# A fused attention and MLP kernel: casting loads gated on q instead of v, the query indicator on another queue, and small parameter work moved from VectorE to GpSimd

## The chip, the cores and the metric

One core of a Trainium2 chip runs the whole kernel. The metric is the device time of one execution in microseconds (us). The engines are TensorE (PE, with its weight loads shown apart as PEld), VectorE (DVE), ScalarE (ACT), GpSimd (POOL) and SyncE (SP); each works through its own instructions in order and waits for others by semaphores. DMAs are issued from the queues of SP, ACT and GpSimd. Only DMAs issued from GpSimd change a type on the way here ("casting loads", float32 in memory to bfloat16 or float16 on chip); those from SP and ACT copy as is.

## The reference

Attention with a block mask over q, k and v of shape [4, 8, 768, 64], then a residual MLP over the result, seen as x of shape [4, 768, 512]:

```python
scores = scale * np.matmul(q, k.transpose(0, 1, 3, 2))
# mask: neighbouring blocks of 32, first and last block, three sampled blocks per block row
scores = np.where(mask, scores, -1000000000.0)
attn = softmax(scores)
x = heads side by side of np.matmul(attn, v)
a1 = alpha1 * x + beta1
u = x + lam * (w_tok @ a1)          # over the 768 positions
a2 = alpha2 * u + beta2
out = u + lam * (np.maximum(a2 @ w_ch1, 0.0) @ w_ch2)
```

## The kernel before, in words

The work is cut into 16 pairs of heads (4 batches, 4 pairs each). A pair has 9 units; a unit is a set of score matmuls for 128 keys by 512 queries twice (line 576, `emit_qk`), one exponential over 128x1024 on ACT (line 594, `emit_exp`), and the product of the exponentials with v on PE (line 623, `emit_pv`). The score tile `sp` has two buffers, so the scores of unit s wait for the exponential of unit s-2.

For the first 5 pairs the mask is part of the score matmul: below the 64 rows of q stand 24 rows that tell the block of each query (the **query indicator**, `indq_c`, loaded by DMA into `qTs` at lines 350 and 362), and below the 64 rows of k stand 24 rows of a mask term (`kTs`, lines 426 and 432: `emit_mask_part` and the copies `rows1` to `rows3`). No score matmul can run before the indicator has landed in its buffer. Later pairs multiply by `mask01`, which GpSimd builds piece by piece (line 512).

The order is written out. A loop over the first 45 units (line 1012) emits, for each step s, the scores, the exponential, at some steps the loads of a later pair, then the small jobs whose date in the table `PLAN` has the whole part s and a fraction below 0.5, then the product with v of unit s-2, then the jobs with a fraction of 0.5 or more. The table `ENG` says on which engine a small copy runs (0 VectorE, 1 ScalarE, 2 GpSimd). After step 45 the strings `WEAVE` give the order. As every engine runs in the emitted order, a date decides what an instruction stands behind.

The start, which the change touches:

- Lines 345 to 364 issue the first DMAs: q, k and v of the first pair, head by head (`load_first`, line 341, 192 KB each), the sampled blocks, the constants (identity and static mask, 80 KB), the query indicator (72 KB, once for each of two buffers) and the rows of lam, alpha1 and beta1 (`vrows`).
- On GpSimd, lines 373 to 380 make `pick` from the identity (it waits for the constants), and line 382 copies one column of the first v into `gate`. This copy does nothing but wait: the casting loads that follow it on GpSimd's queue (`emit_load`, line 304) don't start before that v has landed.
- `emit_parts` (lines 679 to 683) splits the 12 rows of `vrows` into three bfloat16 parts with five small instructions, on VectorE. `emit_bcast` (line 688) multiplies `pick` with the parts on PE, which spreads lam, alpha1 or beta1 over 128 partitions, and VectorE evicts it (lines 697 and 699). These feed `a1pp` (lines 655 and 656) on GpSimd.
- `emit_tps0` transposes q and k of the first pair on PE (line 474), `emit_tps` those of pairs 1 to 4 (line 486); VectorE evicts them (lines 464 and 492). `emit_wtk_load` (line 738) loads the token weights, which PE transposes (line 744) from step 11 on.
- `emit_warm` (line 456) issues PE matmuls on zeros at the start, in the gaps.

Of the kernel before, what the change touches and what calls it, by code (L numbers as in the profile page):

```python
# [16 lines left out]
ALU = mybir.AluOpType  # L17
# [54 lines left out]
]  # L72
WEAVE = W1 + W2 * (B - 2) + W3
ENG = {
    "layv00": 0,
    "layv01": 0,
    "layk01": 0,
    "layq01": 0,
    "kT0": 0,
    "qT0": 0,  # L80
    "kT1": 0,
    "qT1": 0,
    "mp0": 1,
    "mp1": 1,
    "mp2": 0,
    "rows1": 0,
    "rows2": 0,
    "rows3": 0,
    "parts": 0,
    "tk1": 0,  # L90
    "tq1": 0,
}
# [2 lines left out]
    "wtkl": 0.42,  # L95
    "warm1": 0.49,
    "loadv2": 0.58,
    "mask_cols": 1.6,
    "layk01": 1.22,
    "layq01": 1.25,  # L100
    "rows2": 4.5,
    "rows1": 2.08,
    "parts": 2.83,
    "tps0": 2.82,
    "mask1": 2.94,
    "w1_0": 2.96,
    "warm2": 3.04,
    "layv01": 4.3,
    "warm0": 3.31,
    "bcast0": 4.1,  # L110
    "tq1": 3.8,
    "tk1": 4.82,
    "bcast2": 5.12,
    "rows3": 5.84,
    "lv1": 6.01,
    "loadk3": 6.08,
    "loadv3": 6.92,
    "mask3": 7.41,
    "bcast1": 7.8,
    "loadk2": 8.21,  # L120
    "loadq3": 8.23,
    "loadq2": 8.52,
    "a1pp0": 9.37,
    "w1_2": 9.64,
    "w1_1": 10.3,
# [11 lines left out]
    "wt3": 15.31,  # L137
    "columns_use": 16.32,
    "tk2": 16.6,
    "tok0_0": 16.75,  # L140
    "tok0_1": 17.4,
    "tk3": 18.13,
    "loadk4": 18.23,
# [16 lines left out]
    "lv4": 25.4,  # L160
    "tok1_1": 25.6,
    "tok1_2": 27.2,
    "loadv5": 27.51,
    "tok1_3": 27.74,
    "tok1_4": 28.91,
    "tok1_5": 29.7,
# [1 line left out]
    "mask5": 30.09,  # L168
    "tq4": 30.41,
    "mask15": 30.72,  # L170
    "tk4": 30.72,
    "udma0": 31.32,
    "udma1": 31.9,
    "w2_1": 32.0,
    "tq5": 32.01,
    "mask9": 32.65,
    "tok2_0": 33.91,
    "tk5": 34.64,
# [5 lines left out]
    "mask11": 35.79,  # L184
    "tok2_3": 36.37,
    "lam16": 37.24,
    "mask16": 37.75,
    "tok2_4": 37.77,
    "mask10": 37.9,
    "tok2_5": 38.61,  # L190
    "w2_3": 38.7,
    "tok3a_0": 38.84,
    "tok3a_1": 38.93,
    "tok3a_2": 39.02,
    "tok3a_3": 39.35,
    "tok3b_0": 39.51,
    "tok3b_1": 39.52,
    "tok3b_2": 39.53,
    "tok3b_3": 39.54,
    "mask17": 39.68,  # L200
    "ut2": 39.85,
    "tok3a_4": 39.98,
    "mask12": 40.23,
    "tok3b_4": 40.23,
    "usc1": 40.28,
    "lv5": 40.42,
    "tok3a_5": 40.52,
    "ut3_0": 40.8,
    "tok3b_5": 41.21,
    "cast3": 42.22,  # L210
    "lam3": 43.09,
    "ut3_1": 43.63,
    "lam1": 44.85,
    "lam10": 44.92,
    "lam7": 45.27,
    "lam0": 45.32,
    "lam11": 45.58,
    "lam6": 45.9,
    "lam13": 46.09,
    "lam2": 46.25,  # L220
    "lam5": 47.61,
    "lam14": 47.82,
    "lam4": 47.9,
    "lam9": 48.25,
    "lam12": 49.8,
    "lam8": 50.02,
    "lam15": 50.13,
}

# [2 lines left out]
def kernel(  # L232
# [16 lines left out]
    nc = tc.nc  # L249
# [30 lines left out]
    def ptile(shape, dt, name):  # L280
        return pp.tile(shape, dt, name=name, tag=name)
# [4 lines left out]
    def copy_of(name):  # L286
        return (nc.vector.tensor_copy, nc.scalar.copy, nc.gpsimd.tensor_copy)[ENG[name]]

    NVB = 3
    vexts = [ptile([P, 2, NT, D + 1], F16, f"vext{i}") for i in range(NVB)]  # L290
    raws = {}

    def emit_load(i, which="qkv"):
        b, hp = i // NP, i % NP
        for nm, src, dt in (("q", q, BF), ("k", k, BF), ("v", v, F16)):
            if nm not in which or (i, nm) in raws:
                continue
            if nm == "q":
                t = qpads[i % 2][:, D : D + 2 * NT * D].rearrange(
                    "p (w x) -> p w x", w=2  # L300
                )
            else:
                t = ap_.tile([P, 2, NT * D], dt, name=nm + "r", tag=nm + "r", bufs=2)[:]
            nc.gpsimd.dma_start(
                t, src[b, 2 * hp : 2 * hp + 2].rearrange("w (p o) d -> p w (o d)", o=NT)
            )
            raws[(i, nm)] = t
# [18 lines left out]
    identb = const[:, 0:P]  # L326
# [13 lines left out]
    def load_first(nm, src, w, eng):  # L340
        eng.dma_start(  # L341
            raws[(0, nm)][:, w, :], src[0, w].rearrange("(p o) d -> p (o d)", o=NT)
        )
# [2 lines left out]
    load_first("k", k, 0, nc.scalar)  # L346
    nc.sync.dma_start(sampi[0:NBLK, :], sampled_blocks.bitcast(I32))
    nc.scalar.dma_start(const[:], const_dr.ap())
    load_first("v", v, 0, nc.sync)
    nc.sync.dma_start(  # L350
        qTs[0][D : D + NBLK], indq_dr.ap().rearrange("r (w s) -> r w s", w=2)
    )
    load_first("k", k, 1, nc.scalar)
    load_first("q", q, 1, nc.sync)
    load_first("v", v, 1, nc.sync)
# [15 lines left out]
        nc.gpsimd.memset(t[:, QS * D :], 0.0)  # L371

    pick = ptile([P, 12], BF, "pick")
    for m in (32, 64):
        nc.gpsimd.tensor_tensor(
            out=pick[0:96],
            in0=identb[0:96, 0:12] if m == 32 else pick[0:96],
            in1=identb[0:96, m : m + 12],
            op=ALU.add,
        )  # L380
    gate = ptile([P, 1], FP, "gate")
    nc.gpsimd.tensor_copy(out=gate[:], in_=raws[(0, "v")][:, 0, 0:1])
    expb = ptile([P, 1], FP, "expb")
    nc.vector.memset(expb[:], EXPB)

# [2 lines left out]
    for o in (slice(0, 4), slice(4, NT)):  # L388
# [6 lines left out]
        out=eqt,  # L395
        in0=rndf[0:NBLK, :].unsqueeze(2).broadcast_to([NBLK, NR, NBLK]),
        in1=eqt,
        op=ALU.is_equal,
# [8 lines left out]
        out=mbs[0:NBLK, :],  # L407
        in0=mbm[0:NBLK, :],
# [8 lines left out]
    def emit_mask_part(jp, copy):  # L417
        sl = kText[0][D : D + NBLK, ts(jp, 2 * P)]
        dst = sl.rearrange("q (o g r) -> q o g r", o=2, r=16)
        src = mbs[0:NBLK, :].rearrange("q (g m) -> q g m", m=3)  # L420
        m_of = (6 * np.arange(16) + 2 * jp) // BLK
        assert (m_of == (6 * np.arange(16) + 2 * jp + 1) // BLK).all()
        for m in range(3):
            lo, hi = np.searchsorted(m_of, [m, m + 1])
            shape = [NBLK, 2, NBLK // 3, int(hi - lo)]
            copy(
                out=dst[:, :, :, int(lo) : int(hi)],
                in_=src[:, :, m].unsqueeze(1).unsqueeze(3).broadcast_to(shape),
            )
# [241 lines left out]
    parts = ptile([P, P], BF, "parts")  # L671
    part = ptile([P, P], BF, "part")
    rest = ptile([P, P], FP, "rest")
    nc.gpsimd.memset(parts[:], 0.0)

    def emit_parts():
        r = slice(0, 12)
        eng = (nc.vector, None, nc.gpsimd)[ENG["parts"]]
        eng.tensor_copy(out=parts[r], in_=vrows[r])
# [237 lines left out]
            start_mlp(i // NP)  # L917

    emit_load(1)
    emit_mask_part(0, copy_of("mp0"))  # L920
    emit_mask_part(1, copy_of("mp1"))
    emit_tps0(0)
# [192 lines left out]
```

## Time and profile before

| | us |
|---|---|
| median of 3 runs | 308.48 (308.0 to 308.75) |
| the profiled execution | 308.91 |
| its span | 306.7 |
| PE busy in the span | 300.1 |
| ACT busy | 213.5 |
| DVE busy | 200.6 |
| GpSimd busy | 105.1 |
| VectorE's five parts instructions, first to last start | 10.98 to 12.76 |
| score matmuls of the first unit start | 6.71 |

The profile takes one execution. Its page gives each engine's busy time, the chain that ended last, and groups of instructions by line. Queries of the trace give the same for stretches of the span, the instructions in order of time, and, for each wait, who ended it: "A <- B: 0.9, 1, 0.9" says that A's engine sat idle 0.9 us in all, once, at most 0.9, until B. In a row of the table of stretches stand the stretch, its length, the busy time of PE, PEld, DVE, ACT and POOL with the number of instructions, the granted TensorE clock (1.00 throughout), the DMA share and what the DMAs moved. In a row in order of time stand the start, the duration, engine, line, operation, and in brackets the idle time before it and what ended that.

### The profile page before, as it was taken

The numbers are of one execution on the slowest core, as the hardware profiler recorded it, in microseconds if no ns is written. First come the engines' busy times: TensorE is split into PE (matmuls) and PEld (weight loads), VectorE is DVE, ScalarE is ACT, GpSimd is POOL, SyncE is SP. The second block draws the span as 40 slices with busy tenths as digits, with TensorE's granted clock in tenths as the row PEclk, the third lists the DMA queues.
The fourth block names the chain that finished last, engine by engine and source line by source line (L and its number), as shares of the span: only waits on it lengthen the run. The fifth ranks groups of instructions, "written<-read, shape, count | busy, mean of one in ns | idle before, by whom it ended". The sixth has DMA issues, their size and how long they took to land.

```text
span 306.7 us, 7685 instructions
## 1 busy us (share of the span) xinstructions
PE 300.1 (98%) x3225; PEld 188.3 (61%) x3225; DVE 200.6 (65%) x373; ACT 213.5 (70%) x314; POOL 105.1 (34%) x141
## 2 busy tenths in 40 slices
PE   7899999999999999999999999999999999999995
PEld 3577888666575756556665655557565765555543
DVE  4887889889776887478686668477786664000111
ACT  4799998999797946869988565869888521454210
POOL 3759598452252161162434600262222200000000
PEclk9999999999999999999999999999999999999999
DMA  5999999962574299353665995344701023000011
GB/s 182 167 197 204 203 161 164 150 108 42 107 113 84 61 126 204 92 82 82 86 116 108 157 116 85 95 73 73 109 36 26 36 60 89 9 34 34 36 68 68
DMA packets 56293, 31.00 MB, mean 101 GB/s; under 512 B 36352, under 2 KB 53140, under 8 KB 56132
## 3 DMA queue, kind: packets, MB, share of 16 engines
q0 software_dynamic: 16608, 14.22, 31.8%
q1 hardware_dynamic: 39220, 15.83, 24.7%
q8 instruction: 25, 0.41, 0.5%
q10 hardware_dynamic: 432, 0.48, 0.5%
q14 instruction: 8, 0.07, 0.1%
HBM read 29.86 MB, written 6.29 MB: 118 GB/s over the span
## 4 chain that ended last, share of the span: by engine, by line
PE 94%; ACT 2%; DMA 1%; DVE 1%; issue 0%; SPq 0%; DVEq 0%
PE mm L829 27%; PE mm L848 26%; PE mm L761 11%; PE sp L576 11%; PE op L623 11%; PE mm L576 4%; ACT eT L594 2%; DMA qTs<-indq_c 1%; PE mm L868 1%; PE mm L623 1%; PE mm L486 1%; PE mm L744 1%; PE mm L791 1%; SPq L341 0%; DVE qTs L464 0%
## 5 line engine op out<-in xcount | busy, mean ns | idle before, releaser
L594 ACT ACTIVATE eT<-sp,expb 128x1024 f16<-128x1024 f32 x111 | 119.1, 1119 | 6.1 <-PE sp L576 5.7
L836 ACT ACTIVATE hts<-mm 128x384 bf16<-128x384 f32 x128 | 60.7, 498 | 51.7 <-PE mm L829 51.7
L829 PE MATMUL mm<-uT,w1b 128*128 128x384 bf16 x512 | 95.3, 326 | 0.0
L848 PE MATMUL mm<-w2b,hts 128*128 128x512 bf16 x368 | 90.6, 379 | 0.0
L611 DVE TENSOR_TENSOR eT<-eT,mask 128x1024 f16<-128x1024 f16 x99 | 75.8, 780 | 20.5 <-ACT eT L594 20.2
L655 POOL TENSOR_TENSOR a1pp<-x_sb,vbc 128x384 bf16<-128x384 f32 x27 | 29.9, 1107 | 124.9 <-DVE x_sb L641 99.3
L829 PEld LDWEIGHTS <-w1b 128*128 128x128 bf16 x512 | 47.3, 98 | 31.6 <-issue 0.9
L623 PEld LDWEIGHTS <-eT 128*128 128x128 f16 x1152 | 47.5, 98 | 18.6 <-issue 5.0
L594 ACT ACTIVATE eT<-mm,expb 128x512 f16<-128x512 f32 x66 | 41.7, 684 | 19.0 <-PE mm L576 18.9
L848 PEld LDWEIGHTS <-hts 128*128 128x128 bf16 x368 | 33.1, 98 | 32.2 <-issue 1.5
L623 PE MATMUL op<-vext,eT 128*128 128x65 f16 x1008 | 47.4, 194 | 0.1
L857 DVE TENSOR_TENSOR ot<-x_sb,mm 128x512 f32<-128x512 f32 x23 | 15.7, 684 | 41.0 <-PE mm L848 41.0
L761 PE MATMUL mm<-a1pp,wtokT 128*128 128x128 bf16 (+1 forms) x612 | 39.7, 216 | 0.0
L761 PEld LDWEIGHTS <-wtokT 128*128 128x128 bf16 x612 | 34.7, 98 | 4.6 <-ACT hts L836 1.0
L576 PE MATMUL sp<-qTs,kTs 88*128 88x512 bf16 (+1 forms) x120 | 26.9, 325 | 1.3 <-ACT eT L594 0.5
L656 POOL TENSOR_TENSOR a1pp<-a1pp,vbc 128x384 bf16<-128x384 bf16 x27 | 27.2, 1008 | 2.1
L776 DVE TENSOR_TENSOR x_sb<-x_sb,mm 128x384 f32<-128x384 f32 x32 | 17.6, 549 | 11.4 <-PE mm L761 10.8
L576 PE MATMUL sp<-qhT,khT 64*128 64x256 bf16 (+1 forms) x198 | 20.4, 305 | 0.0
L576 PEld LDWEIGHTS <-khT 64*128 64x128 bf16 x264 | 11.3, 94 | 14.7 <-issue 9.2
L782 DVE CAST ubf<-x_sb 128x384 bf16<-128x384 f32 x32 | 17.7, 553 | 1.1
L641 DVE TENSOR_TENSOR x_sb<-op,rcp 128x384 f32<-128x384 f32 x28 | 15.6, 557 | 1.0
L640 DVE RECIPROCAL rcp<-op 128x6 f32<-128x6 f32 x28 | 5.4, 191 | 13.0 <-PE op L623 13.0
(86 smaller groups left out, 184.1 us busy)
## 6 DMA issues: line engine op xcount, KB each, us to landing
out_dram<-ot SPq DMA_DIRECT2D x23, 256.0 KB, 3.0
qpad<-in_q_dram POOLq DMA_DIRECT2D x15, 192.0 KB, 3.8
kr<-in_k_dram POOLq DMA_DIRECT2D x15, 192.0 KB, 5.2
vr<-in_v_dram POOLq DMA_DIRECT2D x15, 192.0 KB, 5.7
w1b<-in_moe_w_ch_dram POOLq DMA_DIRECT2D x4, 512.0 KB, 10.6
w2b<-in_moe_w_ch_dram POOLq DMA_DIRECT2D x4, 512.0 KB, 7.8
hts<-in_moe_w_tok_dram POOLq DMA_DIRECT2D x1, 1152.0 KB, 11.5
x_sb<-in_k_dram ACTq DMA_DIRECT2D x2, 192.0 KB, 3.4
```

The costliest lines, as they stand in the source:

```text
L576: nc.tensor.matmul(sp[jj][:, dst], lhsT, rhs, start=True, stop=True, skip_group_check=True,)
L594: nc.scalar.activation(dst, at, AF.Exp, bias=expb[:], scale=SCALE)
L611: nc.vector.tensor_mul(out=e, in0=e, in1=keep)
L623: nc.tensor.matmul(op[0][:, o, :], ets[u][:, jj, h * QB + n * P : h * QB + n * P + P], vexts[i % NVB][:, w, 2 * jp + jj, :], start=op[1] == 0,
L655: eng.tensor_tensor(out=dst, in0=x_sbs[b][:, :, cols], in1=bc[0], op=ALU.mult)
L656: eng.tensor_tensor(out=dst, in0=dst, in1=bc[1], op=ALU.add)
L761: nc.tensor.matmul(ps[:, o % 3, cols], wtokT[:, os_, ts(o, P)], a1pps[i][:, os_, cols], start=(os_ == 0 and o % 3 == 0 and half != 1), sto ...
L776: nc.vector.tensor_tensor(out=x, in0=x, in1=ps[:], op=ALU.add)
L782: nc.vector.tensor_copy(out=ubfs[i][:, sl, :], in_=x_sbs[b][:, sl, ts(hp, P)])
L829: nc.tensor.matmul(ps[:, 0:QC], w1b[:, dk, ts(n, P)], uTs[b][:, dk, ts(c, QC)], start=(dk == 0), stop=(dk == 3),)
L836: nc.scalar.activation(hts[(b, c)][:, n, :], ps[:, 0:QC], AF.Relu)
L848: nc.tensor.matmul(ps[:], ht[:, nk, ts(o % 3, P)], w2b[:, nk, :], start=(nk == 0), stop=(nk == NH - 1),)
```

## The change

Six things are done:

1. The first query indicator is issued from ACT's queue, third there (after the first k and the constants, ahead of the second head's k), instead of fourth on SP's queue.
2. `gate` copies from the first q instead of the first v.
3. `pick` (two instructions) and the memset of `parts` are emitted after the casting loads of pair 1 instead of before them.
4. The five parts instructions and the copy `rows2` run on GpSimd instead of VectorE.
5. The three broadcasts have their dates one step later, the transposes `tps0` of the second head half a step earlier within step 2, and the copy of pair 1's v (`lv1`) one step earlier.
6. Some dates after step 16 move: the first token job behind the step's products, transposes of pairs 4 and 5 by half a step to one step, some jobs of pairs 2 and 3 by half a step, one load of w2 ahead of pair 6's casting loads, some mask and lam jobs.

The core of the diff:

```diff
     "mp2": 0,
+    "parts": 2,
...
-    "rows2": 0,
+    "rows2": 2,
...
-    "parts": 0,
...
-    "tps0": 2.82,
+    "tps0": 2.52,
     "parts": 2.83,
...
-    "bcast0": 4.1,
-    "bcast2": 5.12,
-    "lv1": 6.01,
+    "lv1": 5.01,
+    "bcast0": 5.1,
+    "bcast2": 6.12,
-    "bcast1": 7.8,
-    "loadq3": 8.23,
+    "bcast1": 8.8,
+    "loadq3": 9.23,
...
-    "tok0_0": 16.75,
+    "tok0_0": 17.05,
...
-    "tk4": 30.72,
+    "tk4": 31.72,
-    "tq5": 32.01,
+    "tq5": 32.51,
...
-    "w2_3": 38.7,
+    "w2_3": 37.7,
...
     nc.scalar.dma_start(const[:], const_dr.ap())
-    load_first("v", v, 0, nc.sync)
-    nc.sync.dma_start(
+    nc.scalar.dma_start(
         qTs[0][D : D + NBLK], indq_dr.ap().rearrange("r (w s) -> r w s", w=2)
     )
+    load_first("v", v, 0, nc.sync)
     load_first("k", k, 1, nc.scalar)
...
-    for m in (32, 64):
-        nc.gpsimd.tensor_tensor(
-            out=pick[0:96],
-            in0=identb[0:96, 0:12] if m == 32 else pick[0:96],
-            in1=identb[0:96, m : m + 12],
-            op=ALU.add,
-        )
     gate = ptile([P, 1], FP, "gate")
-    nc.gpsimd.tensor_copy(out=gate[:], in_=raws[(0, "v")][:, 0, 0:1])
+    nc.gpsimd.tensor_copy(out=gate[:], in_=raws[(0, "q")][:, 0, 0:1])
...
-    nc.gpsimd.memset(parts[:], 0.0)
...
     emit_load(1)
+    for m in (32, 64):
+        nc.gpsimd.tensor_tensor(
+            out=pick[0:96],
+            in0=identb[0:96, 0:12] if m == 32 else pick[0:96],
+            in1=identb[0:96, m : m + 12],
+            op=ALU.add,
+        )
+    nc.gpsimd.memset(parts[:], 0.0)
     emit_mask_part(0, copy_of("mp0"))
```

More of the change, by code (lines that the diff above doesn't have):

```diff
@@ L74 @@
 ENG = {
+    "kT0": 0,
+    "kT1": 0,
+    "layk01": 0,
+    "layq01": 0,
     "layv00": 0,
     "layv01": 0,
[L77 to L82, printed above, removed]
     "mp0": 1,
@@ L85 @@
     "mp2": 0,
+    "parts": 2,
+    "qT0": 0,
+    "qT1": 0,
     "rows1": 0,
-    "rows2": 0,
+    "rows2": 2,
     "rows3": 0,
-    "parts": 0,
     "tk1": 0,
@@ L97 @@
     "loadv2": 0.58,
-    "mask_cols": 1.6,
     "layk01": 1.22,
     "layq01": 1.25,
-    "rows2": 4.5,
+    "mask_cols": 1.5,
     "rows1": 2.08,
+    "tps0": 2.52,
     "parts": 2.83,
-    "tps0": 2.82,
     "mask1": 2.94,
@@ L107 @@
     "warm2": 3.04,
+    "warm0": 3.31,
+    "tq1": 3.8,
     "layv01": 4.3,
-    "warm0": 3.31,
-    "bcast0": 4.1,
-    "tq1": 3.8,
+    "rows2": 4.5,
     "tk1": 4.82,
-    "bcast2": 5.12,
+    "lv1": 5.01,
+    "bcast0": 5.1,
     "rows3": 5.84,
-    "lv1": 6.01,
     "loadk3": 6.08,
-    "loadv3": 6.92,
+    "bcast2": 6.12,
+    "loadv3": 7.02,
     "mask3": 7.41,
-    "bcast1": 7.8,
     "loadk2": 8.21,
-    "loadq3": 8.23,
     "loadq2": 8.52,
+    "bcast1": 8.8,
+    "loadq3": 9.23,
     "a1pp0": 9.37,
@@ L162 @@
     "tok1_2": 27.2,
-    "loadv5": 27.51,
+    "loadv5": 27.53,
     "tok1_3": 27.74,
@@ L170 @@
     "mask15": 30.72,
-    "tk4": 30.72,
-    "udma0": 31.32,
+    "udma0": 30.82,
+    "tk4": 31.72,
     "udma1": 31.9,
-    "w2_1": 32.0,
-    "tq5": 32.01,
+    "w2_1": 32.02,
+    "tq5": 32.51,
     "mask9": 32.65,
@@ L186 @@
     "lam16": 37.24,
+    "mask17": 37.68,
+    "w2_3": 37.7,
     "mask16": 37.75,
@@ L189 @@
     "mask10": 37.9,
-    "tok2_5": 38.61,
-    "w2_3": 38.7,
[L192 to L195, printed above, removed]
+    "tok3a_0": 38.34,
+    "tok3a_1": 38.43,
+    "tok2_5": 38.51,
+    "tok3a_2": 38.52,
+    "tok3a_3": 38.85,
+    "tok3a_4": 39.48,
     "tok3b_0": 39.51,
@@ L199 @@
     "tok3b_3": 39.54,
-    "mask17": 39.68,
     "ut2": 39.85,
-    "tok3a_4": 39.98,
+    "tok3a_5": 40.02,
     "mask12": 40.23,
@@ L206 @@
     "lv5": 40.42,
-    "tok3a_5": 40.52,
     "ut3_0": 40.8,
@@ L210 @@
     "cast3": 42.22,
+    "lam2": 42.25,
     "lam3": 43.09,
@@ L214 @@
     "lam10": 44.92,
+    "lam9": 45.25,
     "lam7": 45.27,
@@ L219 @@
     "lam13": 46.09,
-    "lam2": 46.25,
     "lam5": 47.61,
@@ L223 @@
     "lam4": 47.9,
-    "lam9": 48.25,
+    "lam8": 49.72,
     "lam12": 49.8,
-    "lam8": 50.02,
     "lam15": 50.13,
```

## The prediction

> **What bounds the kernel now.** I read the page first. Its line of busy time puts PE at 300.1 of 306.7 us, and the chain that ended last is PE for 94%. So the span is PE's work plus PE's idle time, and an edit can gain only where PE idles. The second view, the table of stretches, says where that is.
>
> ```profile
> PE 300.1 (98%) x3225; PEld 188.3 (61%) x3225; DVE 200.6 (65%) x373; ACT 213.5 (70%) x314; POOL 105.1 (34%) x141
> ```
> ```profile
> core 0: us, PE busy (x) PEld busy (x) DVE busy (x) ACT busy (x) POOL busy (x), PEclk, DMA share, GB/s
> 0.00:4.60 4.60, 3.41 (x8) 1.04 (x8) 0.85 (x5) 1.73 (x3) 0.94 (x12) 1.00 0.53 166
> 4.60:6.71 2.11, 1.69 (x10) 0.88 (x9) 1.95 (x8) 1.24 (x7) 0.71 (x4) 1.00 0.82 267
> ...
> 8.50:10.81 2.31, 2.12 (x14) 1.05 (x14) 1.80 (x6) 2.31 (x3) 2.31 (x5) 1.00 1.10 163
> 10.81:13.19 2.38, 1.44 (x27) 1.17 (x28) 2.19 (x7) 1.55 (x2) 1.87 (x3) 1.00 1.21 168
> 13.19:15.79 2.60, 2.43 (x38) 1.85 (x39) 2.53 (x6) 1.38 (x3) 0.70 (x1) 1.00 0.97 199
> 15.79:20.29 4.50, 4.03 (x54) 2.76 (x54) 4.25 (x10) 4.50 (x5) 1.67 (x3) 1.00 1.11 199
> 20.29:30.00 9.71, 9.71 (x161) 8.03 (x160) 7.19 (x17) 8.90 (x9) 9.44 (x12) 1.00 1.27 204
> ```
>
> Length less PE busy is PE's idle time. From 20.29 on it is nothing until the last 6.7 us. Between 4.60 and 20.29 it is 0.42, 0.09 (the row left out), 0.19, 0.94, 0.17 and 0.47, together 2.28 us: the most that this change can win, since the end of the kernel is not touched. The third view, the waits of the first 30 us, names two of these by cause, and ACT's loss beside them.
>
> ```profile
> ACT eT L594 <- PE sp L576: 3.7, 6, 1.2
> ...
> PE mm L688 <- DVE parts L683: 0.9, 1, 0.9
> ...
> PE sp L576 <- DMA qTs<-indq_c: 0.4, 1, 0.4
> ```
>
> The fourth view, the instructions in order of time, shows the two places: the first score matmuls at 6.71 come 0.42 us late for the query indicator; the broadcast at 13.19 waits for five small DVE instructions that begin at 10.98, and the next scores (13.99) stand behind it, so that ACT, idle from 13.40, begins its sixth exponential only at 14.63.
>
> ```profile
> 6.71 0.59 PE L576 MATMUL sp<-qTs,kTs 88*128 88x512 bf16 x2 [0.42 <-DMA qTs<-indq_c]
> ...
> 10.98 0.21 DVE L679 CAST parts<-vrows 12x128 bf16<-12x128 f32 x1
> ...
> 12.29 1.11 ACT L594 ACTIVATE eT<-sp,expb 128x1024 f16<-128x1024 f32 x1 [0.82 <-PE sp L576]
> ...
> 13.19 0.38 PE L688 MATMUL mm<-parts,pick 96*128 96x128 bf16 x4 [0.94 <-DVE parts L683]
> ...
> 14.63 8.18 ACT L594 ACTIVATE eT<-sp,expb 128x1024 f16<-128x1024 f32 x8 [1.23 <-PE sp L576]
> ```
>
> Eight exponentials then run end to end to 22.81: there ACT paces PE, and afterwards PE is full.
>
> **The change, part by part.**
>
> *Query indicator on ScalarE's queue.* SP issued it fourth at 2.08; ACT issues it third, in the slot that began at 1.67. The last landing moves from 6.67 to at most 6.26 by the issue alone, and earlier if it no longer stands behind the first v (192 KB). PE's two warm-up matmuls end at 6.29 and the weight load had begun at 6.10, so PE starts there: gain 0.42. ACT's queue pays one more issue of 0.40 to 0.48, which puts its table load at 2.65 to 3.93; the cast behind it waited for k until 4.16, so 0.23 of cover is left. The second head's k is issued 0.48 later; its cast is not before 7.44, and the first k took 3.4 us from issue to landing, so it is there near 5.6 plus the 72 KB now ahead of it. SP's later DMAs each move up by about 0.4.
>
> *Parts to GpSimd, broadcast 0 behind the sixth scores.* DVE loses 0.21+0.28+0.59+0.56+0.28 = 1.92 us, plus one rows copy of 0.35. On PE the order becomes scores 4, values, k transposes, scores 5, broadcast 0. Before, from 11.65: scores 4, stall, broadcast, values (8 matmuls), transposes, scores 5 ending at 14.59. Now, everything 0.43 earlier: scores 4 at 11.22, done 11.82; the pieces take 0.43, 0.25 and 0.34 on PE by the chain, so scores 5 begin near 12.24 and are done at 12.84. Exponential 4 starts at 11.86 and lasts 1.11 to 12.97; exponential 5 follows at once. It was at 14.63: **1.66 us earlier**, of which 0.42 is the indicator, 0.94 the stall, and about 0.30 the broadcast's own PE time, now under ACT-paced scores. The broadcast's work of 0.24 to 0.38 moves into 12.7 to 21, where PE had 0.64 of idle time for it.
>
> *Do the parts come in time?* GpSimd before: gate at 6.21, then three casting loads 0.89, 0.71, 0.71 apart, the token weights 0.55, three loads at 0.70 each, the mask copy at 11.45. Now the gate waits for q, which DVE's first cast got at 3.99. The loads go out from about 4.15; picks (0.29 each), memset, weights and three loads follow, and the parts start at 9.8. No row has these five on GpSimd. Low bound: 0.20 each as the 96x12 add, 1.0 in all. High: 1.1 each as the 128x384 multiply, 5.5. Nearest rows are the mask copy (240 elements, 0.60) and that multiply scaled to 128 columns: 0.38 for the three copies and 0.55 for the two subtractions, 2.25 in all, done at 12.1. PE wants them at 12.7. A later finish costs nothing until 12.9 (broadcast 0.24, values 0.25, scores 0.6, against exponential 6 at 14.0); from there it costs one for one. The end runs from 10.8 to 15.3, so the cost from 0 to 2.4.
>
> [...]
>
> *Gate on q.* The three loads go out 2.3 us earlier; they landed no sooner than 3.8, 4.1 and 5.6 us after issue, so pair 1 is in by about 8.0, 9.2 and 11.4, against PE's wants at 10.9 (q) and 11.9 (k) and DVE's near 14 (v). The token weights took 11.5 us and PE waited 0.16 for them at 20.29. They are issued at 7.15 instead of 8.78 and stand behind data that is 2.2 earlier: landing 18.1 to 18.7, and PE's want moves to 18.5. So this part gains nothing by itself; it keeps the weights from taking back the 1.66. Their possible cost is 0 to 0.2.
>
> *Rows 2 on GpSimd.* 768 columns, 0.8 to 2.0 us by the same rows, after the first w1 issue: done by 16 at the latest, wanted by the tenth scores near 17. GpSimd had waited 1.78 and 3.46 us at 12.7 to 18.6, which hides this and the parts. *Values 1 a step earlier, and dates after step 16* (token jobs, transposes of pairs 4 and 5 by half a step to a step, one w2 load ahead of pair 6's loads): PE is full there and no work is added; cost nothing, with the cover that the buffers are written steps ahead; if it fails, a rival below.
>
> **Sum.** 0.42 + 0.94 + 0.30 = 1.66 us. The profiled execution took 308.91 (span 306.7 and 2.2 around it) and would take 307.25. The median of the runs is 308.48, 0.43 below that execution; so the median after is 306.8, rounded to **306.9** for the weights' 0 to 0.2.
>
> **Rivals.** What a measurement of this kernel can tell is about 0.3%, 0.93 us: faster means under 307.55.
>
> 1. *Parts late on GpSimd* (that engine becomes the bound). With the two rows unscaled (three copies at 0.60, two subtractions at 1.1) they take 4.0, end at 13.8 and lose 0.9: 307.8. At the upper bound of 15.3 it is 2.4 and the time 309.3. For: no row shows these operations, and each waits for the one before. Against: GpSimd's 0.20 us rows for small tiles.
>
> 2. *Casting loads crowd out the first head: slower.* Before, the first bytes of these loads show about 1.8 us after the first issue (the table by microseconds has 43 GB/s in 8 to 9, 192 after); now that is near 6.0, when the direct loads still had 162 and 76 KB to move in 6 to 7 and 7 to 8. If shared evenly, the second head's q is up to 0.8 late, its transposes at 9.1 instead of 8.5, and 0.5 is lost (307.4). If the casting loads go first, q waits towards their landing at 11.4, the transposes begin near 12.3, 3.8 late, and the time is 306.9 + 3.8 = 310.7. It turns slower by over 0.3% once those transposes are more than 2.6 us late, past 11.1. Against: the direct loads are issued by 4.2, ahead of the casts.
> [...]
>
> 3. *The later dates give it back.* PE has no slack from 20.29 to 300, so a job moved past its consumer stalls it 1:1. To take all 1.6 back a new wait of that size must appear in 20 to 60; the time is 308.5. Against: the ACT and DVE queues keep nearly the same order there.
>
> 4. *The indicator lands no earlier*, since the same DMA engines carry it: 1.24 gained, 307.3.
>
> **Chances.** Forecast 0.66 (306.3 to 307.4), rival 1 0.12 (307.3 to 309.3), rival 2 0.07, rival 3 0.10, rival 4 0.05. Faster: 0.66 + 0.05 + 0.06 of rivals 1 to 3 in their mild forms = 0.77. Slower: 0.04 of rival 2 and 0.03 of the ends of 1 and 3 = 0.07. Same: 0.16. The range goes from 306.1 (all 2.28 won) to 308.2 (most of rival 1), leaving out under 2 in 10.
>
> **What would show it.** The first score matmuls start at 6.3 with no wait for the indicator; exponential 5 starts near 13.0 and ACT has no gap of a microsecond after it; the broadcast waits under 0.3 for the parts, whose last GpSimd row ends by 12.9; the first token-weight transpose is near 18.6; PE idle between 4.6 and 20 sums to about 0.6. Wrong would be: a wait of PE's broadcast on GpSimd over 0.5, DVE idle before the second head's casts, or new PE idle time between 20 and 60.

## The result and the profile after

| | before | after |
|---|---|---|
| median of runs in one series, us | 308.85 (308.0 to 309.81, 6 runs) | 306.31 (306.2 to 306.68, 6 runs) |
| the profiled execution, us | 308.91 | 306.68 |
| its span, us | 306.7 | 304.7 |

The ratio after to before is 0.9918, with the interval 0.9897 to 0.9938: 1.9 to 3.2 us faster, by the medians 2.5. The forecast was 306.9 with a range of 306.1 to 308.2.

The page's line of busy time: PE lost 0.7 us of busy time while the span lost 2.0, so most of the gain is PE's idle time. VectorE has six instructions fewer, GpSimd six more.

```profile
PE 299.4 (98%) x3225; PEld 188.2 (62%) x3225; DVE 197.3 (65%) x367; ACT 213.4 (70%) x314; POOL 109.0 (36%) x147
```

The table of stretches of the kernel after, cut as in the prediction:

```profile
core 0: us, PE busy (x) PEld busy (x) DVE busy (x) ACT busy (x) POOL busy (x), PEclk, DMA share, GB/s
4.60:6.71 2.11, 2.11 (x11) 1.06 (x11) 1.98 (x8) 1.26 (x7) 2.08 (x3) 1.00 0.84 259
...
8.50:10.81 2.31, 2.12 (x20) 1.08 (x19) 1.79 (x5) 2.31 (x3) 2.23 (x5) 1.00 1.25 195
10.81:13.19 2.38, 2.38 (x48) 2.09 (x45) 1.47 (x3) 1.56 (x3) 2.12 (x6) 1.00 0.98 197
13.19:15.79 2.60, 2.19 (x30) 1.46 (x28) 2.52 (x5) 2.60 (x4) 2.50 (x5) 1.00 1.04 213
15.79:20.29 4.50, 4.22 (x69) 3.39 (x68) 3.69 (x9) 4.49 (x6) 3.25 (x5) 1.00 1.18 186
```

Length less PE busy is now 0, 0.10 (the row left out), 0.19, 0, 0.41 and 0.28: together 0.98 us where it was 2.28. The stretch from 10.81 to 13.19, which held the stall of 0.94, is full. Where PE still idles, from 13.19 on, ACT is busy all the time (2.60 of 2.60, 4.49 of 4.50): the idle time left belongs to ACT's pace.

The waits of the first 30 us of the kernel after:

```profile
ACT eT L587 <- PE sp L569: 2.4, 4, 0.8
...
PE sp L569 <- ACT eT L587: 0.7, 2, 0.4
```

PE's waits for the parts (0.9) and for the indicator (0.4) are gone, and none for the token weights has come. ACT waits for scores 1.3 us less. The instructions in order of time of the kernel after (line 569 is 576 before, 587 is 594, 671 to 675 are 679 to 683, 680 is 688, 736 is 744):

```profile
6.15 0.97 PE L569 MATMUL sp<-qTs,kTs 88*128 88x512 bf16 x2
...
10.11 0.28 POOL L671 CAST parts<-vrows 12x128 bf16<-12x128 f32 x1
...
11.66 0.42 POOL L675 TENSOR_TENSOR parts<-rest,part 12x128 bf16<-12x128 f32 x1
...
12.11 3.13 ACT L587 ACTIVATE eT<-sp,expb 128x1024 f16<-128x1024 f32 x3 [0.82 <-PE sp L569]
...
12.93 0.39 PE L680 MATMUL mm<-parts,pick 96*128 96x128 bf16 x4
...
18.86 0.84 PE L736 MATMUL mm<-const,hts 128*128 128x128 bf16 x12
```

The broadcast at 12.93 has no wait in its row, the parts end at 12.08, and from 12.11 ACT runs the fifth, sixth and seventh exponentials end to end (numbers 4 to 6 in the count from 0 that is used below). But the first pair of score matmuls takes 0.97 us where it took 0.59 before; the last section comes back to that.

**Where the 2.23 us between the two profiled executions lie.** I count from exponential to exponential, by ScalarE's activations numbered from 0. Up to 40 these are all exponentials; later the count takes in ScalarE's evictions for the MLP (line 836 before, 828 after), so that its number 113 is the exponential that starts at 108.88 before and at 106.94 after:

| from, to | before | after | gained |
|---|---|---|---|
| start of the span to exponential 0 | 7.34 | 7.16 | 0.18 |
| exponential 0 to 13 | 15.62 | 14.33 | 1.29 |
| exponential 13 to 40 | 31.02 | 30.76 | 0.26 |
| exponential 40 to 113 | 54.90 | 54.69 | 0.21 |
| exponential 113 to the end of the span | 197.8 | 197.8 | 0.0 |
| outside the span | 2.2 | 2.0 | 0.2 to 0.3 |

The forecast had the first two rows (0.42 and 1.24) and nothing in the others.

### The profile page after: what moved, and what is told of

It is laid out like the page before. It is cut to its first block, busy times and chain, and to the rows that moved or that the text cites. A ratio compares the mean times of both kernels' runs of the same rounds, so it can differ in the third digit from the quotient of the medians.

```text
span 304.7 us, 7686 instructions
## 1 busy us (share of the span) xinstructions
PE 299.4 (98%) x3225; PEld 188.2 (62%) x3225; DVE 197.3 (65%) x367; ACT 213.4 (70%) x314; POOL 109.0 (36%) x147
## 2 busy tenths in 40 slices
DMA packets 56294, 31.01 MB, mean 102 GB/s; under 512 B 36352, under 2 KB 53140, under 8 KB 56132
## 4 chain that ended last, share of the span: by engine, by line
PE 96%; ACT 3%; issue 0%; DVE 0%
PE mm L821 28%; PE mm L840 26%; PE mm L753 11%; PE op L616 11%; PE sp L569 10%; PE mm L569 4%; ACT eT L587 3%; PE op L449 2%; PE mm L860 1%; PE mm L616 1%; PE mm L479 1%; PE mm L736 1%; PE mm L783 1%; PE mm L467 0%; PE mm L519 0%
## 5 line engine op out<-in xcount | busy, mean ns | idle before, releaser
L768 DVE TENSOR_TENSOR x_sb<-x_sb,mm 128x384 f32<-128x384 f32 x32 | 17.6, 550 | 12.4 <-PE mm L753 12.1
```

Source lines behind the costliest of these rows:

```text
L768: nc.vector.tensor_tensor(out=x, in0=x, in1=ps[:], op=ALU.add)
```

## The experiments

The theory was that of the prediction: the stall and the broadcast's place ahead of the sixth scores make the main gain, and the gate on q only keeps the token weights from taking it back. The rivals put the gain down to the parts' move off VectorE, to the indicator, or to the later dates. The first three kernels do one part alone on the kernel before, the fourth does two together; of those behind the row of after, the first four take one part out of the kernel after, and the last four are about what was left over. No kernel takes the gate alone out of the kernel after, and the smaller moves at the start (`pick`, `tps0`, `lv1`) were not run by themselves. "exp 0 to 13" and the like are the stretches of the table above.

| kernel | exp 0 at | 0 to 13 | 13 to 40 | 40 to 113 | execution | ratio of medians (interval) |
|---|---|---|---|---|---|---|
| before | 7.34 | 15.62 | 31.02 | 54.90 | 308.91 | 1 |
| indq_only | 7.13 | 15.11 | 31.02 | 54.92 | 308.31 | 0.9984 (0.9967 to 1.0002) |
| bcast_only | 7.42 | 15.58 | 31.02 | 54.91 | 308.94 | 0.9975 (0.9956 to 0.9994) |
| gate_only | 7.39 | 15.05 | 31.02 | 54.91 | 308.38 | 0.9967 (0.9950 to 0.9985) |
| bcast_gate | 7.17 | 14.33 | 31.02 | 54.91 | 307.45 | 0.9951 (0.9929 to 0.9972) |
| after | 7.16 | 14.33 | 30.76 | 54.69 | 306.68 | 0.9918 (0.9897 to 0.9938) |
| after_bcast_early | 6.67 | 15.03 | 30.77 | 54.69 | 306.91 | 0.9930 (0.9911 to 0.9950) |
| after_parts_dve | 7.17 | 14.48 | 30.78 | 54.91 | 307.49 | 0.9941 (0.9922 to 0.9960) |
| after_indq_sp | 7.20 | 14.33 | 30.79 | 54.69 | 306.58 | 0.9921 (0.9903 to 0.9939) |
| after_old_late | 6.75 | 14.33 | 31.01 | 54.70 | 306.51 | 0.9923 (0.9904 to 0.9942) |
| after_pad_dve8 | 6.62 | 14.33 | 30.77 | 55.33 | 306.78 | 0.9930 (0.9915 to 0.9945) |
| parts_dve_pad_pool10 | 6.91 | 14.59 | 30.78 | 54.90 | 306.87 | 0.9929 (0.9917 to 0.9942) |
| after_less_warm | 6.90 | 14.02 | 30.78 | 54.69 | 306.12 | 0.9907 (0.9895 to 0.9920) |
| after_less_warm_tq1 | 6.61 | 14.17 | 30.78 | 54.69 | 305.96 | 0.9902 (0.9888 to 0.9916) |

The columns are the reading. Exponential 0 moves about from execution to execution (6.61 to 7.42), much of it with the moment at which TensorE's matmuls reach their full pace, for which the last section has the figures. The three stretches behind it repeat to 0.03 us between kernels that share the part at stake, but for the two with the parts back on VectorE (14.48 and 14.59). Two cautions go with them. Each kernel has one profiled execution. And a stretch that holds a wait for something with a date of its own, GpSimd's parts or a DMA, grows when exponential 0 comes early; that concerns after_bcast_early and the last two kernels. Single parts differ by less than the intervals of their medians, so the medians confirm only the sums.

### The broadcast a step later, alone

```diff
-    "bcast0": 4.1,
+    "bcast0": 5.1,
-    "bcast2": 5.12,
+    "bcast2": 6.12,
-    "bcast1": 7.8,
+    "bcast1": 8.8,
```

> The kernel before with only the dates of the three broadcasts one step later; the five parts instructions stay on VectorE, the gate on v. Theory 1: the sixth scores no longer stand behind the broadcast's wait, so the sixth exponential starts near 13.3 instead of 14.63, but PE reaches the first token-weight transpose near 19 and waits over 1 us for weights that land at 20.3: total gain 0.0 to 0.3, with a wait of 1 us or more on that DMA. Theory 2: 1.2 to 1.3 us gained in all, no such wait. A third view, that VectorE's parts work itself is the delay: the sixth exponential does not come before 14.2, as VectorE's transposes copies stand behind the parts.

Measured: 308.38 against 308.95, and a span of 306.7 as before. Exponential 5 starts 1.24 us earlier (13.39), exponential 13 does not (23.00 against 22.96). The waits of this kernel say what took the gain:

```profile
PEld L744 <- DMA hts<-in_moe_w_tok_dram: 1.3, 1, 1.3
...
PE mm L744 <- DMA hts<-in_moe_w_tok_dram: 1.0, 1, 1.0
```

PE now waits 1.0 us for the token weights, where it had waited 0.16. In this execution the gain was real and was given back 7 us later. It is the second slowest of twelve, though: the median is 0.57 below that of before, and the interval, 0.9956 to 0.9994, leaves out 1. So over many executions part of the gain seems to stay; when the weights landed in the others isn't recorded.

### The gate on q, alone

```diff
-    nc.gpsimd.tensor_copy(out=gate[:], in_=raws[(0, "v")][:, 0, 0:1])
+    nc.gpsimd.tensor_copy(out=gate[:], in_=raws[(0, "q")][:, 0, 0:1])
```

> The kernel before with only the gate copied from q instead of v (the picks stay ahead of it). Both theories: the casting loads go out about 1.5 us earlier, the token weights land near 18.8 instead of 20.29, PE does not wait for them, and the total moves by 0 to 0.2 us, as nothing wants the loads earlier. Rival (casting loads crowd out the first pair's direct loads): VectorE waits for the second head's q and k, and the time is longer by 0.3 to 0.8 us.

Measured: 308.23, and 0.57 less from exponential 0 to 13 in its profile. By the prediction this part gains nothing by itself. The rows of this kernel in order of time:

```profile
10.23 0.58 POOL L512 COPY mask<-maskt 128x240 f16<-128x240 f16 x1
...
11.83 0.21 DVE L681 CAST part<-rest 12x128 bf16<-12x128 f32 x1
12.07 0.22 DVE L682 CAST parts<-rest 12x128 bf16<-12x128 f32 x1
```

The two casts on VectorE took 0.59 and 0.56 before, when GpSimd's mask copy began at 11.45, and take 0.21 and 0.22 now that this copy begins at 10.23 and is over at 10.81. The first cast, at 11.04, is slowed in their place: 0.44 where it took 0.21, beside the issue of a casting load (10.64 to 11.43). All five end at 12.60 instead of 13.04, so the parts' stall of 0.94 was partly a slowed VectorE: the broadcast's wait for the parts is 0.44 here. In the trace of before the first slowed cast began at 11.54, behind the copy's start, and ended at 12.13, the copy at 12.05. The second was beside the issue of a casting load and ended at 12.72, the issue at 12.68. In bcast_only the cast that began together with the copy, at 11.63, took 0.21, and the next one ended at 12.32, the copy at 12.25. So the slowed casts of these three traces end 0.04 to 0.08 behind what GpSimd does beside them. Not every cast beside GpSimd is slowed: the first one of before, at 10.98, took 0.21 beside the issue of a casting load (10.74 to 11.50). By what way GpSimd holds up VectorE is not shown.

### Both together

The two diffs above in one kernel.

> Both of the last two edits together: broadcasts one step later and the gate on q; parts still on VectorE, indicator still on SP's queue. Theory 1: now the earlier sixth exponential is not given back to the weights: total gain 1.0 to 1.3 us, although each edit alone gives 0 to 0.3. Theory 2: the sum of the two alone. If the parts on VectorE cost something by themselves (2 us of its time ahead of the copies of transposes), the gain stays under 0.8.

Measured: 307.65; 14.33 from exponential 0 to 13, the same as the whole change to 0.01 us. Alone the parts give 0.04 and 0.57, together 1.29. That is the main result: these two edits, three numbers and one letter of the diff, make the whole gain of this stretch. That each needs the other is less sure: by the medians of twelve runs each the single edits gain 0.57 and 0.72 and the pair 1.30, which is their plain sum. So the 1.3 for the pair is shown both ways, its split only for the profiled executions. From here to the kernel after, profile to profile, another 0.77 remain: 0.26 from 13 to 40, 0.22 from 40 to 113, and 0.27 outside the span.

### The indicator third on ScalarE's queue, alone and undone

```diff
-    load_first("v", v, 0, nc.sync)
-    nc.sync.dma_start(
+    nc.scalar.dma_start(
         qTs[0][D : D + NBLK], indq_dr.ap().rearrange("r (w s) -> r w s", w=2)
     )
+    load_first("v", v, 0, nc.sync)
```

> The kernel before with one edit: the first query indicator goes out third on ScalarE's queue. Theory 1 (parts depend on each other): the first scores start at 6.15 as in the changed kernel, but PE's 512-column matmuls are still 0.43 us apart there instead of 0.215, so the first exponential starts at 7.16 and not at 6.9: 0.18 us earlier, not 0.42. PE then runs into the token weights, which landed at 20.29 before and are not moved here, so that even the 0.18 is lost there: total gain 0.0 to 0.2. Theory 2 (each part adds its own gain, as the sum of the prediction had it): 0.42 us.

Measured: 308.57 against 308.95, an interval that reaches 1.0002. The profiled execution gains 0.7 of span, more than I had expected, and most of it not at exponential 0 (0.21) but from 0 to 13 (0.51). With the indicator off SP's queue the first v is there sooner: the gate's copy, still on v, runs at 5.33 instead of 6.21, and with it the mask copy at 10.61 instead of 11.45. So the two casts take 0.24 and 0.22, as with the gate on q: in this execution the edit acts as a second way to open the gate earlier.

The same edit taken back in the kernel after:

> The changed kernel with the first query indicator back as the fourth DMA of SP's queue. Theory 1: the first scores start 0.3 to 0.6 us later (6.5 to 6.8), but at PE's full rate if that has come by then, so the first exponential starts 0 to 0.25 later than at 7.16 and the total is 0 to 0.25 longer. Theory 2: 0.42 longer.

Measured: 306.62 against the 306.31 of after, ratios 0.9921 and 0.9918, not to be told apart. The row of the first scores shows the wait again, with the indicator as its cause:

```profile
6.53 0.62 PE L569 MATMUL sp<-qTs,kTs 88*128 88x512 bf16 x2 [0.25 <-DMA qTs<-indq_c]
```

Exponential 0 starts at 7.20, 0.04 behind that of after, although the scores started 0.38 later. The scores' two matmuls took 0.62 here and 0.97 in after: TensorE's pace, told in the last section. One effect of the edit shows in every run, outside the span: 1.75 to 1.80 us here against 1.87 to 1.98 in the six runs of after, and 2.29 to 2.41 in the twelve of indq_only against 2.16 to 2.28 in the 35 of before. So the indicator on ScalarE's queue costs about 0.13 us there; why isn't shown.

### The broadcasts at their old dates in the kernel after

The diff of the broadcast turned round.

> The changed kernel with the three broadcasts at their old dates, so that broadcast 0 stands ahead of the values and the sixth scores again; the parts stay on GpSimd, where they end at 12.1. Theory 1: PE reaches the broadcast near 11.9, waits 0.2 to 0.3 for GpSimd, and the sixth exponential comes near 13.6 to 13.7 instead of 13.1: 0.4 to 0.6 us longer than the changed kernel, so the order of PE is worth half a microsecond and the engine of the parts the rest of 1.5. If the place of the parts alone made the gain, the time is that of the changed kernel within 0.15; if it made nothing, 1.2 or more longer.

Measured: 306.94. From exponential 0 to 13 it takes 15.03, 0.70 more than after; the profiled execution shows only 0.23 of it, as exponential 0 came 0.49 earlier: the first scores began at 6.04 and took 0.59, where in after they began at 6.15 and took 0.97. Its rows:

```profile
12.01 0.38 PE L680 MATMUL mm<-parts,pick 96*128 96x128 bf16 x4 [0.42 <-POOL parts L675]
...
13.45 2.12 ACT L587 ACTIVATE eT<-sp,expb 128x1024 f16<-128x1024 f32 x2 [0.71 <-PE sp L569]
```

GpSimd's parts alone don't remove the stall in this execution: PE waits 0.42 for them in place of 0.94, and the sixth exponential again waits for scores, 0.71. But the parts end at 11.96 here and at 12.08 in after, although exponential 0 is 0.49 earlier: they follow GpSimd's work and not PE's. Had PE come 0.49 later, as in after, it would have found them ready (an estimate from these rows). So 0.70 is the most that these profiles give, and the 0.21 by which exponential 13 is later (21.70 against 21.49) the least; the intervals of the two medians overlap (0.9911 to 0.9950 and 0.9897 to 0.9938). The place of the broadcast counts from this side too, by an amount between the two.

### Parts and rows 2 back on VectorE

```diff
-    "parts": 2,
+    "parts": 0,
-    "rows2": 2,
+    "rows2": 0,
```

> The changed kernel with the parts and the copy of rows 2 back on VectorE. Theory 1: the broadcasts stand behind the sixth scores anyway, VectorE is done with the parts near 12.4, and ACT paces PE from there: same as the changed kernel within 0.15 us. Theory 2 (the move to GpSimd takes 1.9 us out of VectorE's work ahead of PE): 0.3 to 1 us longer, with scores of pair 1 waiting for VectorE's copies.

Measured: 307.20. The profiled execution is 0.81 slower than after: 0.16 by exponential 13, 0.22 from 40 to 113, 0.41 outside the span. Only the first of these is what the move was thought to be about. The other two lie 90 and 290 us behind the moved instructions; the pads below go after them.

### The dates after step 16 as before

```diff
-    "tk4": 31.72,
+    "tk4": 30.72,
...
-    "tq5": 32.51,
+    "tq5": 32.01,
...
-    "w2_3": 37.7,
+    "w2_3": 38.7,
...
```

(18 dates in all, from tok0_0 to lam8.)

> The changed kernel with the 18 dates after step 16 set back to those of the kernel before. The prediction's view: PE is full from 20 us on, the dates cost and bring nothing: same time as the changed kernel within 0.1 us. Theory 1 as the traces now suggest (a busy PE is not a PE without waits): the changed kernel's gain grew from 1.47 us at the fourteenth exponential to 1.72 at the first MLP matmul and 1.95 after 103 us, and a kernel with the old dates and the early edits kept 0.5 less: so this one is 0.4 to 0.5 us longer than the changed kernel, with the loss between 35 and 55 us and near 103 us.

Measured: 306.53, and 31.01 from exponential 13 to 40 where after has 30.76: the dates are worth 0.25 us, all of it there. Measured from exponential 13, the tables of stretches of both kernels agree up to about 40 us; the gain lies between there and 52 us, where PE is busy all the time in both, so it sits inside rows that count as busy. I did not locate it further. The execution as a whole is 0.17 faster than that of after only because its exponential 0 came 0.41 earlier: the two matmuls ahead of it took 0.59 (from 6.12), where they took 0.97 (from 6.15) in after. These stand ahead of all the moved dates.

### Idle instructions as pads

Eight memsets, each of one column of an unused tile, at the start of VectorE's work in the kernel after; ten on GpSimd in the kernel with the parts on VectorE. They compute nothing that is used.

```diff
     nc.vector.memset(expb[:], EXPB)
+    pad = ptile([P, 8], FP, "pad")
+    for n in range(8):
+        nc.vector.memset(pad[:, n : n + 1], 0.0)
```

> The changed kernel with eight memsets of one column added on VectorE at the start, where it waits for q; they compute nothing that is used. Every kernel with the parts on VectorE (eight records more) loses 0.22 us near 103 us, at a score matmul that waits for VectorE's add, and none with the parts on GpSimd does. Theory 1 (VectorE's instruction count shifts a stall there): the 0.22 comes back near 103 us though the parts stay on GpSimd, and the span is 0.2 longer. If the parts' place itself matters there: no such loss, the changed kernel's time within 0.15 us.

Measured: 306.76. The loss near 102 us came back. The same rows of the kernel before, of after, and of this one, with VectorE's add (`x_sb<-x_sb,mm`) ahead of them:

```profile
102.68 0.55 DVE L776 TENSOR_TENSOR x_sb<-x_sb,mm 128x384 f32<-128x384 f32 x1
...
103.05 0.61 PE L576 MATMUL mm<-qhT,khT 64*128 64x512 bf16 x2
...
103.29 0.80 PE L576 MATMUL sp<-qhT,khT 64*128 64x256 bf16 x6
```
```profile
100.74 0.55 DVE L768 TENSOR_TENSOR x_sb<-x_sb,mm 128x384 f32<-128x384 f32 x1
...
101.31 0.40 PE L569 MATMUL mm<-qhT,khT 64*128 64x512 bf16 x2
...
101.54 0.60 PE L569 MATMUL sp<-qhT,khT 64*128 64x256 bf16 x6
```
```profile
100.84 0.55 DVE L771 TENSOR_TENSOR x_sb<-x_sb,mm 128x384 f32<-128x384 f32 x1
...
101.21 0.61 PE L572 MATMUL mm<-qhT,khT 64*128 64x512 bf16 x2
...
101.45 0.80 PE L572 MATMUL sp<-qhT,khT 64*128 64x256 bf16 x6
```

The pair of matmuls on 64 rows takes 0.40 in after, and 0.61 with the eight idle instructions, as it did before. All kernels with the parts on VectorE have 0.61 to 0.63, all with the parts on GpSimd 0.40 but for the padded one. So 0.2 us here come and go with instructions of VectorE that stand some 90 us ahead. The rows show where. In all fourteen traces the second matmul of the pair starts 0.05 us after VectorE's add ends (103.28 and 103.23 before, 101.34 and 101.28 in after, 101.45 and 101.40 here), as it would if it waited for the buffer of `mm` that the add reads. The add itself starts 0.61 after the start of the mask multiply ahead of it in after, and 0.82 in the kernels with the loss, where VectorE stands idle for 0.13 or 0.14 in between. What holds it in that gap is not shown. The pad has a second effect that I had not expected and can't explain: 55.33 from 40 to 113 is 0.43 more than before, of which a PE wait at 52.11 (0.25, for nothing that the profile shows) is part.

The ten on GpSimd:

> The kernel with the parts back on VectorE (all else as changed), with ten memsets of one column added on GpSimd while it waits for q at the start; they compute nothing that is used. That kernel took 307.2 (median) with 2.4 us of its profiled execution outside the span, the changed one 1.98. In all kernels with the parts on VectorE an 8 KB instruction fetch falls after the last instruction, in those with the parts on GpSimd the same fetch is at 239 us with GpSimd near its 197th record, and none at the end. Theory 1 (the number of GpSimd's instructions decides where its last fetch falls): with ten more, the fetch moves to near 240 us, the time outside the span goes down to 1.8 to 2.0 and the median to 306.8 or less, though nothing useful was changed. If the fetch has nothing to do with it: 307.2 within 0.15.

Measured: 306.81, where the unpadded kernel had 307.20 in its own series; the profiled executions are 306.87 and 307.49, and outside the span they spend 1.9 and 2.4. The intervals of the two medians overlap, but the time outside the span does not: 1.87 to 1.94 in the six runs with the pad, 2.36 to 2.42 in the six without. The views of the DMA queues show one candidate. In the kernel before, from 300 us to the end:

```profile
q14 instruction: 1, 0.01, 0.4%
```

In the kernel after, from 230 to 245 us:

```profile
q14 instruction: 1, 0.01, 0.2%
```

Each is the only packet of that queue of instructions in its stretch. The late one starts at 307.7 in the kernel before, 1.0 us behind the last instruction. All six kernels with it after 300 us spend 2.2 to 2.4 us outside the span; all eight with it near 240 spend 1.8 to 2.0, the padded one among them, whose parts are on VectorE. So about 0.5 us outside the span hang on the number of GpSimd's instructions, which moves that packet; from before to after 0.3 of it are left, as the indicator costs 0.13 there. That the packet is the cause fits all fourteen kernels but is not shown by itself.

### Two warm-up matmuls fewer

The parts end 0.85 us before the broadcast begins, so the start had room. `warm0` and `warm2`, single matmuls on zeros, are left out; nothing that the output needs.

```diff
-        "warm0": lambda: emit_warm(1),
+        "warm0": lambda: None,
...
-        "warm2": lambda: emit_warm(1),
+        "warm2": lambda: None,
```

> The changed kernel without the two single warm-up matmuls behind the fourth scores (0.43 us of PE at full rate, no output changes). Theory 1 (PE is ahead of ACT only where it has no useless work): the fifth exponential starts 0.4 us earlier (11.7 for 12.1 in a run whose clock comes at the same time) and the whole kernel is 0.3 to 0.4 us faster. Rival: PE's full rate depends on them, and matmuls of 512 columns go back to 0.43 us apart: 0.5 us or more slower. Second rival: the token weights, landed near 18.1, or ACT cap it: 0 to 0.2 faster.

Measured: 306.12, and 14.02 from exponential 0 to 13, 0.31 less than after. The broadcast's row:

```profile
12.37 0.38 PE L680 MATMUL mm<-parts,pick 96*128 96x128 bf16 x4 [0.41 <-POOL parts L675]
```

PE is early enough here for the parts on GpSimd to be its bound, 0.41. This is the first rival of the prediction, in a mild form and only because PE came earlier. The pace stayed: the two score matmuls at 9.06, the next over 512 columns, took 0.59. The second kernel also moves the transposes `tq1` behind the fifth scores (date 4.45 instead of 3.8):

> The last edit, and the q transposes of pair 1 behind the fifth scores instead of ahead of them. Theory 1: the fifth exponential follows the fourth without a gap, 0.8 us earlier than in the changed kernel; PE has then about 0.6 us less to lose, as the weights' landing near 18.1 comes to be its bound: 0.4 to 0.8 us faster than the changed kernel, the best of all. Rival: VectorE's copies of the transposes come too late for the scores of pair 1, and it is no faster than the last one.

Measured: 305.96, 14.17 from exponential 0 to 13.

```profile
10.38 0.38 PE L569 MATMUL sp<-qTs,kTs 88*128 88x256 bf16 x2 [0.22 <-DVE qTs L457]
```

The scores now wait 0.22 for a copy of VectorE. It is not the one that the rival named: line 457 copies the first pair's second head, and the fifth scores come to it early now that the warm-up matmuls and `tq1` no longer stand ahead of them. The stretch is 0.15 longer, not shorter; that the execution is 0.16 faster is exponential 0, 0.29 earlier. The dates of `tq1` bring nothing that these runs show. Both kernels have lower medians than after, but the intervals of the ratios overlap.

## Why the prediction was right, point by point

- **The stall and the broadcast's own time (0.94 + 0.30 = 1.24 us).** Right: exponential 0 to 13 fell by 1.29, and the place of the broadcast and the gate make all of it (bcast_gate, 14.33).
- **The gate on q keeps the weights from taking it back.** Right in the profiled executions, and the most useful step: alone, the broadcast's move lost its whole gain to them there (1.0 of new wait, PE), though its median kept 0.57. That the gate gains nothing by itself was wrong: it gains 0.57 on the kernel before, with GpSimd's mask copy over at 10.81, ahead of the two casts on VectorE that then took 0.21 and 0.22 instead of 0.59 and 0.56. In the whole change this is not additional, as the stall that it shortens is gone anyway.
- **The indicator, 0.42.** The mis-sized term: 0.18 in the pair of profiles. The scores did start 0.56 earlier (6.71 to 6.15), but they ran at a slower pace (0.97 for two, where 0.59 had been) and lost 0.38 again. Medians can't tell it from nothing (0.9918 with, 0.9921 without). What it brings depends on TensorE's pace: 0.59 at exponential 0 where the first scores already ran at the full one, 0.59 for two (6.75 in after_old_late, 7.34 before); 0.04 against after_indq_sp, since in after it came at 6.94, when both (6.15 and 6.53) had started. That it also costs 0.13 outside the span was in no term.
- **The parts on GpSimd.** Forecast: 2.25 us in all, done at 12.1. Measured: 0.28 for each copy, 0.42 for each subtraction, 1.97 from first start to last end, done at 12.08. The upper bound of 5.5 was far off; the two nearest rows, scaled by columns, were near for the sum. That the end fits to 0.02 is luck: the parts started 0.3 later than forecast (10.11 for 9.8) and took 0.3 less. A subtraction took 0.42 there against VectorE's 0.28, 1.5 times as long, and a copy 0.28 against the 0.21 of VectorE's copies that were not slowed. For the start the move was hardly needed: parts done at 12.39 on VectorE were early enough in bcast_gate, and in the kernel after, taking it back costs 0.15 from exponential 0 to 13.
- **"PE is full there and no work is added; cost nothing."** They cost nothing, but they gained 0.26, which by this reasoning could not be. PE's busy time was 100% in both kernels of the comparison, so full by the busy time does not mean without loss; near 102 us the padded kernel shows such a loss, a pair of matmuls that is longer and counted as busy. What the later dates gain lies elsewhere, between 40 and 52 us, and its cause stays open.
- **The sum.** 1.66 was forecast for exponential 5 (it was 1.50) and taken as the whole. The execution gained 2.23, as 0.26 came from the dates and some 0.5 (0.21 near 102 us, 0.2 to 0.3 outside the span) from instruction counts, which the forecast had no term for. The mechanism of the start was right. Its gain, 1.47 by exponential 13, fell 0.19 short, and these terms added some 0.75; that the total stays in the range is partly luck. PE's idle time from 4.6 to 20 us, forecast at about 0.6, sums to 0.98.
- **The rivals.** No casting load held back the first head: VectorE's casts of the second head began at 7.56 without a wait. Parts late on GpSimd appeared only when PE had been made earlier. The indicator did land earlier.

## What to carry to other kernels

When a stall is removed, list what arrives next and when: here the token weights stood 1 us behind, and in the profiled execution they took back all that the first edit had gained. Measure such edits from one fixed event to another inside the trace, since the start of the first exponential alone moved by 0.8 us between executions and hid terms of 0.2 to 0.7; but look for waits in the stretch that keep a date of their own, and hold one profiled execution against the median of many. And where instructions moved from one engine to another, 0.2 us near 102 us and 0.5 outside the span came and went here, far from the edit, with their mere number; pad with idle instructions before crediting such a gain to the mechanism.

## What the runs showed of the hardware that was not expected

**TensorE reaches its pace at a moment of its own.** At the start, matmuls over 512 columns begin 0.43 us apart, and later 0.215. The moment of the change lay between about 4.2 us (after_pad_dve8, where the eight warm-up matmuls from 1.19 took 3.35 instead of the 3.60 of after) and about 7 us (gate_only, where the two scores at 6.52 took 0.84 and the next two matmuls, at 7.19, took 0.60) in the profiled executions, an estimate from these rows, with nearly the same work on PE. The two kernels that differ only in late dates show it; after's row is above (0.97 at 6.15), this is after_old_late:

```profile
6.12 0.59 PE L569 MATMUL sp<-qTs,kTs 88*128 88x512 bf16 x2
```

So exponential 0 starts between 6.61 and 7.42. The column of the granted clock says 1.00 in the stretches of the start, before and after, and does not show it: the traces of both hold no record of the clock ahead of the full one, and the column counts that as 1.00. The first record begins at 6.48 us before and at 6.94 in after, and the spacings go with it: before, matmuls over 512 columns start at 5.23 and 5.66, 0.43 apart, and then at 6.71 and 6.92, 0.215 apart; in after at 6.53 and 6.96, 0.43 apart, and then at 7.18, 0.22 later. What sets the moment is not shown by these runs.

**Casts on VectorE beside GpSimd.** A cast of 12x128 took 0.21 us with nothing on GpSimd beside it (gate_only, 11.83), and 0.59 where it began 0.09 behind the start of GpSimd's copy of 0.60 and ended 0.08 behind its end (before, 11.54). One that began together with such a copy (bcast_only, 11.63) took 0.21. Beside the issue of a casting load one took 0.44 (gate_only, 11.04) and one 0.21 (before, 10.98).

**Two matmuls on 64 rows each**, one reading partitions 0 to 63 and one 64 to 127, took 0.40 us as a pair over 512 columns in after, at 101.31, where the second one starts 0.03 behind the first, and 0.61 to 0.63 in the kernels that lose 0.2 there, where it starts 0.24 behind (before, 103.05). The page of the profile counts both as busy.

**What stays open:** what delays VectorE's add near 102 us; where the later dates gain their 0.26; the 0.4 us at 52 us in the padded kernel; whether the late packet of instructions itself costs the 0.5 us; when the token weights land in executions that were not profiled; and what the indicator is worth over many executions.
